# Order of the first projections: keys and queries ahead of values in the opening of a fused attention and gated-MLP kernel

## The chip, the cores and the metric

The kernel runs on one core of one Trainium2 chip. The metric is the device time of one execution in microseconds (us). The kernel before takes 264.70 us, the median of four runs (264.58 to 265.78 us). The profile comes from one further execution of the same kernel, which took 264.69 us; its span, from the first to the last instruction, is 262.9 us.

## The reference

Two branches, both fed with the normalised input, are added to the input; there are 2048 tokens of width 512:

```
xn  = layernorm(x)                              # 2048 x 512, no weights
q,k,v = xn @ wqkv                               # 32 heads of 16
s   = q k^T / 4, masked to 0 <= i - j < 256     # sliding window of 256 tokens
att = softmax(s) v @ wo
glu = ((xn @ w_gate) * (xn @ w_up)) @ w_down    # 512 -> 1792 -> 512
out = x + att + glu
```

All tensors are bf16; sums are kept in f32.

## The kernel before, in words

Tokens are worked in four chunks of 512 (`T` = 0 to 3), each of four blocks of 128 (`b`). For a chunk the kernel needs the normalised tokens transposed (`xnT`, model dimension on the partitions), keys, queries and values from `Wqkv`, 14 pairs of gate and up tiles, 15 or 20 batches of scores (exponentials on ScalarE, masks on GpSimd or VectorE), four groups of attention sums, and the sum of `Wd` and `Wo` products for the output.

TensorE (PE) writes to four PSUM banks `M0` to `M3` for everything but scores, and to `S` for scores. It works in four shapes of tile, which the trace names: 128*128 (dense products and transposes), 32*128 (scores, line 229), 64*17 (attention sums, line 259) and 128*64 (values, line 707).

The order of the instructions on every engine is not written out by hand. A planner in Python (class `Kernel`, `loop` at line 342, `choose` at line 373, `do` at line 433) runs while the program is built: it keeps a list `A` of dense pieces (class `Dense`, line 37: a name, a number of matmuls, what it depends on, a function that emits it and one that queues its copy out of PSUM), a list `B` of output sums, and counters for scores and attention sums. It estimates when each is ready, and emits the next one. It looks at the first `WINDOW` = 4 pieces of `A` (line 399), adds `SWITCH` = 0.11 when the tile shape would change (line 403), prefers a transpose ("turn") by 0.5 when it is ready soon (line 404), and starts an attention group between dense pieces under a rule with the age `now - 4` (line 389). Other engines' work (`Op`, line 26) is placed by `loop`, with a handicap `HOLD` before the first scores (line 351). So a changed cost or list can change the order of the whole program, though not the work.

The opening (`prologue`, line 150, and `first_chunk`, line 592) is special. Two queues load: ScalarE's x block 0 and two halves of a third of `Wqkv`; SyncE's x block 1, the other halves, then x block 2, 512 KB of `Wqkv`, x block 3, and everything later. `Wqkv` is 1536 columns wide: queries at 0, keys at 512, values at 1024. Loaded first are the values' columns, then the keys', then, behind x block 2, the queries'. Meanwhile 42 idle matmuls (`keep_busy`, line 207) run on PE. For each block VectorE takes the statistics (line 607, 609), ScalarE the square root (616), VectorE the reciprocal (619) and the normalised block `xn` (287); PE transposes it (640), and a copy brings it to `xnT` (647). Then PE makes, block by block, values (`add_v`, line 699), keys and queries (`project`, line 652: 16 matmuls of 128 columns each). Keys leave PSUM in two passes, one for each half of the heads' lanes (`i_keys`, line 290), queries and values in one.

Of the kernel before, what the change touches and what calls it, by code (L numbers as in the profile page):

```python
# [18 lines left out]
SWITCH = 0.11  # L19
# [17 lines left out]
class Dense:  # L37


    def __init__(self, name, mms, deps, emit, evac, mode="D"):  # L40
        self.name, self.mms, self.deps, self.emit, self.evac, self.mode = name, mms, deps, emit, evac, mode


# [47 lines left out]
class Kernel:  # L91
# [4 lines left out]
    PACE = 2.9  # L96
    SHARE = 1.0
    FEED = 0.1
    HOLD = 0.2

    def __init__(self, live=True):
        self.live = live
# [47 lines left out]
    def prologue(self):  # L150
        nc = self.nc
        xv = self.x_d.rearrange("(t p) d -> p t d", p=128)
        w = {k: v.rearrange("(k p) n -> p k n", p=128) for k, v in self.w_d.items()}

        def load(eng, dst, src):
            eng.dma_start(out=dst, in_=src)

        def qkv(eng, lo, k0, k1):
            load(eng, self.Wqkv[:, k0:k1, lo:lo + 512], w["qkv"][:, k0:k1, lo:lo + 512])

        load(nc.scalar, self.x[:, 0, :], xv[:, 0, :])
        load(nc.sync, self.x[:, 1, :], xv[:, 1, :])
        qkv(nc.sync, 1024, 0, 2)
        qkv(nc.scalar, 1024, 2, 4)
        qkv(nc.scalar, 512, 2, 4)
        qkv(nc.sync, 512, 0, 2)
        load(nc.sync, self.x[:, 2, :], xv[:, 2, :])
        qkv(nc.sync, 0, 0, 4)
        load(nc.sync, self.x[:, 3, :], xv[:, 3, :])
        h = self.F // 2  # L170
        for lo in (0, h):
            load(nc.sync, self.Wg[:, :, lo:lo + h], w["g"][:, :, lo:lo + h])
            load(nc.sync, self.Wu[:, :, lo:lo + h], w["u"][:, :, lo:lo + h])
            if lo == 0:
                load(nc.sync, self.x[:, 4:8, :], xv[:, 4:8, :])
        load(nc.sync, self.x[:, 8:NT, :], xv[:, 8:NT, :])
        for f, g in ((0, 5), (5, 10), (10, 14)):
            load(nc.sync, self.Wd[:, f:g], w["d"][:, f:g])
        load(nc.sync, self.Wo[:], w["o"])
        for _ in range(4):  # L180
            nc.sync.drain()

        c = self.const
        nc.gpsimd.memset(self.ident[:], 0.0)
        nc.gpsimd.affine_select(out=self.ident[:], in_=self.ident[:], compare_op=ALU.not_equal, fill=1.0,
                                base=0, pattern=[[-1, 128]], channel_multiplier=1)
        nc.gpsimd.memset(self.mhalf[:], -0.5)
        warm = c.tile([128, 1], F32, name="warm")
        nc.vector.memset(warm[:], 0.0)
        nc.vector.memset(self.eps[:], 1e-5)  # L190
        nc.scalar.activation(out=warm[:], in_=warm[:], func=ACT.Sqrt)
        self.warm = warm
        pi = c.tile([128, 1], I32, name="pi")
        nc.gpsimd.iota(pi[:], pattern=[[0, 1]], base=0, channel_multiplier=1)
        podd = c.tile([128, 1], I32, name="podd")
        nc.vector.tensor_scalar(out=podd[:], in0=pi[:], scalar1=4, scalar2=1,
                                op0=ALU.arith_shift_right, op1=ALU.bitwise_and)
        nc.vector.tensor_copy(out=self.own[:, 1:2], in_=podd[:])
        nc.vector.tensor_scalar(out=self.own[:, 0:1], in0=podd[:], scalar1=0, scalar2=None, op0=ALU.is_equal)
        nc.gpsimd.memset(self.V[0][:, :, :, 16:18], 1.0)  # L200
        for _ in range(4):
            nc.vector.drain()
        self.keep_busy(42, 0)

# [168 lines left out]
    def choose(self):  # L373

        now = self.now
        s = v = None
        more = self.g < len(self.batches)
        if more:
            s = early = self.when(self.score_deps(self.g))
            if s is not None and self.first_s is not None:  # L380
                s = max(s, self.first_s + self.PACE * self.g)
        free = sorted((t, i) for i, t in enumerate(self.banks) if t is not None)
        near, ready = False, None
        if self.v < len(self.pairs):
            near = self.of_pair[self.v][-1] < self.g
            v = ready = self.when(self.value_deps(self.v))
            if v is not None:
                v = max(v, free[1][0]) if len(free) > 1 else None
        if v is not None and v + 0.15 <= now and (self.mode == "S" or not more or s is None or s > now + 1.5 or v < now - 4):
            return now, "V", None  # L390
        if s is not None and s <= now:
            return now, "S", None
        cands = []
        if s is not None:
            cands.append((max(s, now), "S", None))
        if v is not None and (not more or s is None):
            cands.append((max(v, now), "V", None))
        a = b = None
        for n, d in enumerate(self.A[:self.WINDOW]):
            t = self.when(d.deps)  # L400
            if t is not None and free:
                t = max(t, free[0][0], now)
                t += SWITCH * (d.mode != self.mode) + SWITCH * (d.mode == "C" and self.mode == "D")
                t -= 0.5 * (d.name.startswith("turn") and t <= now + 0.4)
                if a is None or t < a[0]:
                    a = (t, n)
        if self.B and (self.B[0].T < NCH - 1 or not self.A):
            d = self.B[0]
            t = self.when(d.deps)
            if t is not None and ("bank" in d.link or free):  # L410
                b = max(t, now if "bank" in d.link else max(now, free[0][0]))
        held = near and len(free) < 3 and ready is not None and ready <= now + self.SOON
        if a is not None and held and (b is not None or cands):
            a = None
        if a is not None and b is not None:
            left = sum(x.hi - x.lo for x in self.B if x.T < NCH - 1)
            if max(a[0], b) <= now:
                kind = "B" if self.credit >= 1 and not left <= 5 else "A"
            else:
                kind = "A" if a[0] <= b else "B"  # L420
        else:
            kind = "A" if a is not None else "B" if b is not None else None
        if kind == "A":
            d = self.A[a[1]]
            a = (max(now, free[0][0], self.when(d.deps)), a[1])
            cands.append((a[0], "DA", a[1]))
        elif kind == "B":
            cands.append((b, "DB", None))
        if s is not None and early < s <= now + self.LEAD:
            cands.append((max(early, now) + 0.03, "S", None))  # L430
        return min(cands, key=lambda x: x[0]) if cands else None

    def do(self, at, kind, what):
        if at > self.now + 0.005:
            self.idle.append((self.now, at - self.now, kind))
        mode = self.A[what].mode if kind == "DA" else kind[0]
# [6 lines left out]
            self.do_values(at)  # L443
        elif kind == "DA":
            d = self.A.pop(what)
            i = self.take_bank()
            o = self.pe(at, d.mms * MM, d.name)
            if self.live:
                d.emit(i)
# [1 line left out]
            b = sum(x.hi - x.lo for x in self.B if x.T < NCH - 1)  # L451
            self.credit += d.mms * self.SHARE * b / max(sum(x.mms for x in self.A), 30)
        else:
            d = self.B[0]
# [136 lines left out]

    def first_chunk(self):

        land = (3.35, 3.4, 7.5, 9.6)
        wv, wk, wq = 5.6, 6.9, 9.2
        nc = self.nc
        roots = []
        for b in range(4):
# [9 lines left out]
                if n == halves - 1:  # L608
                    nc.vector.bn_aggr(out=self.mv[0][:, b, :], in_=keep["st"][:, 0:halves, :])  # L609

            deps = [land[b]]
            for n in range(halves):
                took = (0.72 if halves == 1 else 0.38) + (0.14 if n == halves - 1 else 0)
                s = self.op(f"st{b}", {"V": (took, took + 0.04)}, deps, lambda e, n=n, bn=bn: bn(e, n), rank=0.5)
# [20 lines left out]
        for b in range(4):  # L635
# [13 lines left out]
                self.at_["xnT", 0, b] = self.at_["xnT", 0, b, ks.start] = x  # L649
                x.then.append(lambda o: self.at_.update({("begun", 0, b, ks.start): o.start}))  # L650

            def project(i, lo, tok=tok):
                for k in range(4):
                    for c in range(4):
                        self.nc.tensor.matmul(  # L655
                            self.M[i][:, 128 * c:128 * c + 128], lhsT=self.Wqkv[:, k, lo + 128 * c:lo + 128 * c + 128],
                            rhs=self.xnT[0][:, k, tok], start=k + c == 0, stop=k == 3, skip_group_check=True)
# [14 lines left out]
                for c in range(4):  # L672
                    self.at_["Q", 0, c, b] = x

            at = len(self.A) - 2 if b else 0
            for n, ks in enumerate(([0, 1], [2, 3]) if b == 0 else ([0, 1, 2, 3],)):
                self.A.insert(at + n, Dense(f"turn{b}", 1.1 * len(ks) / 4, [("ap", b, n)], lambda i, f=turn, ks=ks: f(i, ks),
                                            lambda o, i, f=turned, ks=ks: f(o, i, ks)))
            self.add_v(0, b, wv)
            self.add(f"k0b{b}", 4.4, [("xnT", 0, b), wk], lambda i, f=project: f(i, 512), k_out)  # L680
            self.add(f"q0b{b}", 4.4, [("xnT", 0, b), wq], lambda i, f=project: f(i, 0), q_out)

    def norms(self, T):
        w = T % 2
# [14 lines left out]
    def add_v(self, T, b, land=0.0):  # L699
# [14 lines left out]
            self.frees(x, i)  # L714
            self.at_["V", T, b] = x

        x = [("xnT", T, b)] if T + b else [("xnT", 0, 0, 0), ("begun", 0, 0, 2)]
        self.add(f"v{T}.{b}", 4, x + [land] + self.ring(T, 2)[:1 if T == 3 else 0], emit, evac, "C")

    def add_qk(self, T, c):  # L720
# [130 lines left out]
```

The softmax here doesn't subtract the row's maximum and nothing guards it: scores larger than these inputs give would overflow.

## Time and profile before

| what | from | value |
|---|---|---|
| median of four runs | times | 264.70 us |
| the profiled execution | times | 264.69 us |
| its span | the page's first line | 262.9 us |
| PE busy | part 1 | 258.6 us, 98% of the span |
| VectorE, ScalarE, GpSimd busy | part 1 | 189.7, 165.4, 119.1 us |
| PE in the chain that ended last | part 4 | 96% |
| granted PE clock | cores | 1.000 |
| first real PE work (transpose of block 0) | timeline | 5.58 us |
| first scores | timeline | 17.03 us |
| last matmuls, end of the span | timeline | 259.9 us, 262.9 us |

Lines of the timeline give the start, the duration, the engine, the source line, the operation, what is written and read with its shape, the number of instructions merged in the line, and in brackets the idle time of that engine before them with what ended it. Matmuls are pipelined: the duration of a line runs to the modelled end of its last matmul, some 0.2 us after the next line may have started. So the pace of PE is read from one start to the next.

### The profile page before, as it was taken

The page shows a single profiled execution, that of the slowest core. Times are in us where ns is not written, and L with a number is a line of the kernel's source. Part 1 is how long each engine was busy: PE and PEld are TensorE (multiplying, and loading weights), DVE is VectorE, ACT ScalarE, POOL GpSimd, SP SyncE. Part 2 cuts the span into 40 slices and gives each one's busy share as a digit, 9 for nine tenths or more (in the row PEclk, how much of TensorE's full clock was granted, in tenths as well). Part 3 has the DMA queues.
Part 4 walks back from the last instruction along what each step waited for, and adds up shares of the span by engine and source line. Part 5 has one row for each costly group of instructions (what it writes and reads, how often), then busy time and mean ns, then how long its engine had stood idle before and what let it go on. Part 6 is the DMA issues. An engine that isn't in the chain of part 4 may idle for free.

```text
span 262.9 us, 8001 instructions
## 1 busy us (share of the span) xinstructions
PE 258.6 (98%) x3456; PEld 131.8 (50%) x3456; DVE 189.7 (72%) x367; ACT 165.4 (63%) x122; POOL 119.1 (45%) x274
## 2 busy tenths in 40 slices
PE   8999999999999999999999999999999999999995
PEld 7974444564444444546444444536535354544562
DVE  4889886969998277787999178777945459787504
ACT  3777676779567675677676756673886765674000
POOL 1046846483183918164282818163073636427000
PEclk9999999999999999999999999999999999999999
DMA  6999910000001300000004200000000100000002
GB/s 214 377 374 350 229 23 1 2 2 1 2 2 42 81 22 22 2 0 2 2 0 82 64 22 0 4 2 0 2 2 22 40 4 22 0 2 0 2 2 82
DMA packets 17252, 13.89 MB, mean 53 GB/s; under 512 B 7104, under 2 KB 17216, under 8 KB 17216
## 3 DMA queue, kind: packets, MB, share of 16 engines
q1 hardware_dynamic: 16384, 12.65, 17.6%
q10 hardware_dynamic: 832, 0.72, 0.8%
q8 instruction: 27, 0.44, 0.7%
q14 instruction: 9, 0.07, 0.1%
HBM read 9.70 MB, written 2.10 MB: 45 GB/s over the span
## 4 chain that ended last, share of the span: by engine, by line
PE 96%; DMA 2%; DVE 1%; issue 0%; ACT 0%
PE M L221 70%; PE S L229 9%; PE M L259 7%; PE M L707 6%; PE M L655 3%; DMA x<-in_A_x_dram 1%; DMA out_dram<-xn 1%; PE S L221 1%; DVE xn L801 1%; PE M L640 1%; DVE st L607 0%; DVE xn L287 0%; ACT ve L616 0%; PE M L211 0%; DVE mv L609 0%
## 5 line engine op out<-in xcount | busy, mean ns | idle before, releaser
L512 ACT ACTIVATE P<-S 128x2048 bf16<-128x2048 f32 x75 | 140.7, 1876 | 57.4 <-PE S L229 49.9
L238 POOL TENSOR_SCALAR_AFFINE_SELECT P<-P 64x256 bf16<-64x256 bf16 (+1 forms) x250 | 112.0, 450 | 111.0 <-ACT P L512 98.8
L221 PE MATMUL M<-xnT,Wu 128*128 128x512 bf16 x224 | 57.7, 380 | 0.0
L221 PE MATMUL M<-xnT,Wg 128*128 128x512 bf16 x224 | 57.7, 380 | 0.0
L221 PE MATMUL M<-Wd,hT 128*128 128x512 bf16 (+1 forms) x224 | 52.3, 373 | 0.0
L759 DVE TENSOR_TENSOR hT<-M,gsb 128x512 bf16<-128x512 f32 x56 | 38.1, 681 | 7.8 <-PE M L221 7.3
L217 DVE CAST gsb<-M 128x512 bf16<-128x512 f32 x44 | 30.2, 686 | 10.8 <-PE M L221 10.6
L221 PEld LDWEIGHTS <-Wu 128*128 128x128 bf16 x224 | 20.4, 98 | 25.2 <-issue 3.0
L221 PEld LDWEIGHTS <-Wg 128*128 128x128 bf16 x224 | 20.5, 98 | 24.8 <-issue 2.1
L221 PEld LDWEIGHTS <-hT 128*128 128x128 bf16 x238 | 21.3, 98 | 23.0 <-issue 2.7
L229 PE MATMUL S<-Q,K 32*128 32x320 bf16 (+4 forms) x720 | 29.9, 254 | 0.0
L550 DVE STREAM_TRANSPOSE at<-M 128x512 f32<-128x512 f32 x32 | 21.4, 699 | 11.6 <-PE M L259 11.4
L229 PEld LDWEIGHTS <-K 32*128 32x128 bf16 x720 | 12.0, 92 | 31.4 <-issue 30.2
L244 DVE TENSOR_TENSOR P<-P,masks 128x512 int16<-128x512 int16 x56 | 22.3, 404 | 5.8 <-ACT P L512 5.8
L221 PE MATMUL M<-xnT,Wqkv 128*128 128x512 bf16 x96 | 22.6, 380 | 0.0
L259 PE MATMUL M<-P,V 64*17 64x320 bf16 (+4 forms) x1440 | 19.5, 252 | 0.0
L801 DVE TENSOR_TENSOR y<-M,x 128x512 bf16<-128x512 f32 x12 | 8.2, 684 | 14.4 <-PE M L221 14.4
L259 PEld LDWEIGHTS <-V 64*17 64x17 bf16 x1440 | 17.0, 86 | 2.6 <-issue 0.8
L298 DVE TENSOR_SCALAR K<-M,own 128x512 bf16<-128x512 f32 x23 | 16.6, 742 | 2.3 <-PE M L221 1.6
L221 PE MATMUL M<-Wo,OT 128*128 128x512 bf16 (+1 forms) x64 | 15.9, 373 | 0.0
L707 PE MATMUL M<-Wqkv,xnT 128*64 128x256 bf16 x256 | 15.5, 274 | 0.0
L707 PEld LDWEIGHTS <-xnT 128*64 128x64 bf16 x256 | 13.4, 110 | 1.8 <-issue 1.5
(53 smaller groups left out, 146.7 us busy)
## 6 DMA issues: line engine op xcount, KB each, us to landing
Wg<-in_B_w_gate_dram SPq DMA_DIRECT2D x2, 896.0 KB, 9.8
Wu<-in_B_w_up_dram SPq DMA_DIRECT2D x2, 896.0 KB, 11.7
out_dram<-y SPq DMA_DIRECT2D x12, 128.0 KB, 1.7
Wd<-in_B_w_down_dram SPq DMA_DIRECT2D x2, 640.0 KB, 12.4
x<-in_A_x_dram SPq DMA_DIRECT2D x1, 1024.0 KB, 13.7
Wqkv<-in_A_wqkv_dram ACTq DMA_DIRECT2D x2, 256.0 KB, 5.1
Wqkv<-in_A_wqkv_dram SPq DMA_DIRECT2D x2, 256.0 KB, 4.7
Wqkv<-in_A_wqkv_dram SPq DMA_DIRECT2D x1, 512.0 KB, 6.3
```

The source lines that it names most:

```text
L217: self.nc.vector.tensor_copy(out=out, in_=in_)
L221: self.nc.tensor.matmul(ps, lhsT=a, rhs=b, start=first and n == 0, stop=last and n == len(pairs) - 1)
L229: self.nc.tensor.matmul(self.S[:, e, 64 * at:64 * (at + m)], lhsT=self.K[U % 3][rows, c, j].rearrange("p l t -> p (l t)"), rhs=self.Q[T % ...
L238: self.nc.gpsimd.affine_select(out=v, in_=v, pattern=[[0, 4], [0, n], [sign, 64]], base=0, fill=0.0, compare_op=ALU.is_gt if kind else ALU ...
L244: self.nc.vector.tensor_tensor(out=v, in0=v, in1=m, op=ALU.bitwise_and)
L259: self.nc.tensor.matmul(banks[lane][32 * e:32 * e + 17, 64 * q:64 * (q + m)], lhsT=self.V[U % 3][rows, j, 4 * c + e, 0:17], rhs=P[rows, e, ...
L298: self.nc.vector.tensor_scalar(out=out, in0=in_, scalar1=own, scalar2=None, op0=ALU.mult)
L512: ex = self.op(f"exp{g}", {"A": (took + 0.06, took + 0.18)}, [o], lambda e: self.nc.scalar.activation(out=P[:, :, 0:hi], in_=self.S[:, :, ...
L550: t = self.op(f"tr{v}", {"V": (0.63, 0.71)}, [o] + ts, lambda e, par=par: nc.vector.transpose(out=self.at[:, :, par, :], in_=self.M[banks[ ...
L707: self.nc.tensor.matmul(self.M[i][64 * lane:64 * lane + 64, 256 * jj:256 * jj + 256], lhsT=self.xnT[T % 2][:, k, tok], rhs=w[:, lane], sta ...
L759: x = self.op(f"u{T}.{f}", {"V": PSUM_COPY["V"]}, [o, ("gate", T, f)], lambda e: self.nc.vector.tensor_tensor(out=self.hT[T % 2][:, f, :], ...
L801: self.nc.vector.tensor_tensor(out=keep["y"][:, cols], in0=self.M[i][:, cols], in1=self.x[:, t, cols], op=ALU.add)
```

## The change

It reorders the loads and the pieces of the opening, and changes the planner's rules:

- Loads: the first third of `Wqkv` on the two queues is now the keys', the second the queries', both in halves; the values' 512 KB go behind x block 2 on SyncE's queue. Sizes and places in the queues stay as they were.
- Pieces: keys and queries of a block are emitted as two half pieces of 8 matmuls that share a bank (`link`). The list is now: keys and queries of blocks 0 and 1, values of 0 and 1, keys and queries of 2 and 3, values of 2 and 3, each transpose ahead of its block's keys.
- Planner: `HOLD` 0.2 to 0.3; the transposes' window 0.4 to 0.2; the age for an attention group 4 kept as `LATE`; the extra cost of entering the 128*64 shape kept as `ENTER` = 0.11; a window of seven pieces before the first scores; a new rule `stays`, which puts scores off by up to 1.2 while value pieces are ready.
- Estimates of landing times, and one `drain` fewer on VectorE, nine more on GpSimd, all before the first data arrive.

```diff
-        qkv(nc.sync, 1024, 0, 2)
-        qkv(nc.scalar, 1024, 2, 4)
+        qkv(nc.sync, 512, 0, 2)
         qkv(nc.scalar, 512, 2, 4)
-        qkv(nc.sync, 512, 0, 2)
+        qkv(nc.scalar, 0, 2, 4)
+        qkv(nc.sync, 0, 0, 2)
         load(nc.sync, self.x[:, 2, :], xv[:, 2, :])
-        qkv(nc.sync, 0, 0, 4)
+        qkv(nc.sync, 1024, 0, 4)
...
-        for _ in range(4):
+        for _ in range(9):
+            nc.gpsimd.drain()
+        for _ in range(3):
             nc.vector.drain()
...
-        if s is not None and s <= now:
+        if s is not None and s <= now and not (now < s + self.STAY and self.stays(now)):
             return now, "S", None
...
-        for n, d in enumerate(self.A[:self.WINDOW]):
+        for n, d in enumerate(self.A[:self.WINDOW + 3 * (self.first_s is None)]):
...
+    def stays(self, now):
+
+        if self.mode != "C" or not any(t is not None and t <= now for t in self.banks):
+            return False
+        ready = [self.when(d.deps) for d in self.A[:self.WINDOW] if d.mode == "C"]
+        return any(t is not None and t <= now for t in ready)
...
-            at = len(self.A) - 2 if b else 0
+            at, x = len(self.A), [("xnT", 0, b)]
...
-            self.add_v(0, b, wv)
-            self.add(f"k0b{b}", 4.4, [("xnT", 0, b), wk], lambda i, f=project: f(i, 512), k_out)
-            self.add(f"q0b{b}", 4.4, [("xnT", 0, b), wq], lambda i, f=project: f(i, 0), q_out)
+            for name, lo, deps, out in (
+                    ("k", 512, (x if b else [("xnT", 0, 0, 0), ("begun", 0, 0, 2)]) + [wk], k_out), ("q", 0, x + [wq], q_out)):
+                link, key = {}, (name, "half", b)
+                self.add(f"{name}0b{b}", 2.2, deps, lambda i, f=project, lo=lo: f(i, lo, (0, 1)),
+                         lambda o, i, key=key: self.at_.update({key: o.start}), "D", link)
+                self.add(f"{name}0b{b}", 2.2, deps + [key], lambda i, f=project, lo=lo: f(i, lo, (2, 3)), out, "D", link)
+
+            if b % 2:
+                self.add_v(0, b - 1, wv)
+                self.add_v(0, b, wv)
```

## Prediction

> **What bounds the kernel now.** I read the shares and the chain first, then PE's timeline, then VectorE's and the landings of the opening. The page:
>
> ```profile
> span 262.9 us, 8001 instructions
> PE 258.6 (98%) x3456; PEld 131.8 (50%) x3456; DVE 189.7 (72%) x367; ACT 165.4 (63%) x122; POOL 119.1 (45%) x274
> PE 96%; DMA 2%; DVE 1%; issue 0%; ACT 0%
> ```
>
> PE is 96% of the chain. Its own timeline tells whether it ever waits:
>
> ```profile
> 5.58 0.54 PE L640 MATMUL M<-ident,xn 128*128 128x128 bf16 x4 [0.43 <-DVE xn L287]
> 6.33 1.06 PE L707 MATMUL M<-Wqkv,xnT 128*64 128x256 bf16 x16
> 7.38 0.40 PE L640 MATMUL M<-ident,xn 128*128 128x128 bf16 x4
> 7.62 2.84 PE L655 MATMUL M<-xnT,Wqkv 128*128 128x128 bf16 x48
> 10.30 0.39 PE L640 MATMUL M<-ident,xn 128*128 128x128 bf16 x4
> ...
> 12.53 2.84 PE L655 MATMUL M<-xnT,Wqkv 128*128 128x128 bf16 x48
> 15.21 1.03 PE L221 MATMUL M<-xnT,Wg 128*128 128x512 bf16 x4
> 16.07 1.03 PE L221 MATMUL M<-xnT,Wu 128*128 128x512 bf16 x4
> 17.03 0.40 PE L229 MATMUL S<-Q,K 32*128 32x320 bf16 x8
> 17.36 2.81 PE L707 MATMUL M<-Wqkv,xnT 128*64 128x256 bf16 x48
> 20.11 0.40 PE L229 MATMUL S<-Q,K 32*128 32x320 bf16 x12
> ```
>
> The reader is to see starts (first column) that follow each other at the pace of the work, while the second column runs past the next start: 48 matmuls from 7.62 to 10.30, 0.0558 us each, and 48 again from 12.53 to 15.21. After 5.58 no line of PE carries an idle time. I went on to the end: a dense tile of four 512-column matmuls takes 0.864 us in each stage, every change of shape costs the same, and the last matmuls start at 259.6. So PE is full from 7.4 us on. Work on PE can be moved but not hidden, and there is no wait left to remove behind the opening.
>
> One place is held by something else, the second transpose at 7.38: its input is normalised until 7.32.
>
> ```profile
> 6.91 0.41 DVE L287 TENSOR_SCALAR xn<-x,mv,rs 128x512 bf16<-128x512 bf16 x1
> 7.44 0.69 DVE L217 CAST V<-M 128x512 bf16<-128x512 f32 x1
> 9.81 0.41 DVE L287 TENSOR_SCALAR xn<-x,mv,rs 128x512 bf16<-128x512 bf16 x1
> ```
>
> The landings, asked for issue by issue (median us from issue):
>
> ```profile
> Wqkv<-in_A_wqkv_dram ACTq DMA_DIRECT2D x1, 256.0 KB, 4.5
> Wqkv<-in_A_wqkv_dram SPq DMA_DIRECT2D x1, 256.0 KB, 4.1
> Wqkv<-in_A_wqkv_dram ACTq DMA_DIRECT2D x1, 256.0 KB, 5.8
> Wqkv<-in_A_wqkv_dram SPq DMA_DIRECT2D x1, 512.0 KB, 6.3
> ```
>
> Issued at 1.24, 1.26, 1.73 and 2.74, they are in by 5.7, 5.3, 7.5 and 9.0 us.
>
> **What the Trainium skill says.** (1) "TensorEngine Tiling (Array Packing)", Key Properties: changing the tiling mode drains the array. The trace agrees and gives the price: gate to up (15.21 to 16.07) is 0.864 us, up to scores (16.07 to 17.03) 0.959: 0.095 us. Leaving the value shape costs 0.098, leaving the scores 0.093. I take 0.095. (2) "TensorE: Matmul & The Clock Gate", Part 1: the clock falls back after an idle window of about 3.4 us. Here the clock is granted from 4.61 us to the end, across 0.43 us of idling at 5.14. (3) "Trainium Kernel Development and Optimization", Key Constraints: DMAs of all queues share 16 engines. No run here shows whose bytes a slot carries to matter; sizes and order of slots decide.
>
> **The change part by part.** Numbers are against the profiled execution: 264.69 us, a span of 262.9 and 1.8 around it; it lies 0.01 us from the median 264.70.
>
> Loads. Every slot keeps its size, queue and place; only columns change. So I keep the landings: keys 5.3 and 5.7, queries 7.1 and 7.5, values 9.0, x block 3 at 9.4. Nothing is moved past another issue. Cost zero, and the cover is the slack below.
>
> Up to the second transpose. Values of block 0 (1.05 us from 6.33 to 7.38, both shape changes and a wait of some 0.05 in it) give way to keys of block 0: 16 x 0.0558 = 0.893 us, 6.33 to 7.23. The transpose still waits for `xn` at 7.32, as everything ahead of that on VectorE and ScalarE is in the same order. It starts at 7.38 again, after 0.15 us idle. Gain zero; if the cover of that wait were gone, 0.155 us gained.
>
> From the second transpose on. PE's work of the opening that is left was 3 blocks of values and 8 of keys or queries; now it is 4 and 7. A value block in a row is (2.744 - 0.098)/3 = 0.882 us, a key block 0.893: -0.01 us. What remains is shape changes. I counted them in the trace's order and in the order the changed program is built in. Before: opening dense, scores, 3 values, scores: 3 changes to the second batch of scores. After: dense to the value pair (between transposes 3 and 4), back, to scores, to the two other values, to a dense tile, to scores: 6. Through the rest the planner's new rules cost +1: in the second chunk an attention group now follows scores directly (-1), in the third one stands between dense tiles (+1), and ahead of the last chunk a dense tile comes between values and scores (+1). Whole program: 173 changes before, 175 after; two of the 173 lay ahead of the second transpose, where they were free, none of the 175. So +4 changes, 4 x 0.095 = +0.38 us.
>
> Do the moved pieces find their inputs? By row: third transpose at 7.38 + 0.23 + 2.68 = 10.30; values from 10.30 + 0.22 + 0.095 = 10.61, which need the columns of 9.0 (slack 1.6); fourth transpose at 10.61 + 2 x 0.882 + 0.098 = 12.48; 64 key and query matmuls of blocks 2 and 3 from 12.70; gate tile at 16.27, scores at 18.09. Block 2's `xn` must be ready by 10.24. VectorE: a key pass (0.74) instead of the values' copy (0.69) from 7.44, statistics to 8.97, then, new ahead of the reciprocal, the queries' copy (0.66) to 9.6, reciprocal at 9.5, `xn` 9.7 to 10.1. ScalarE: `xnT` to 8.42, second key pass (0.69) to 9.04, root to 9.3. That leaves 0.1 us; bounds 0 and +0.3 (one pass of 0.69 not hidden by 0.4), I take 0. Block 3's `xn` ends by the same rows at 12.25 against 12.42. Queries of the second block wait for a 256 KB half at its fifth matmul, 7.84, against 7.54. Block 3's `xnT` copy moves from ScalarE to VectorE: no row has it there; nearest are 0.24 (half as wide) and 0.69; it has 1.6 us until its keys start, so zero. The exponentials' table load (1.28) sits between two query copies of which the second ends near 17.2, 0.8 ahead of the scores.
>
> Later order. The scores come 1.06 us later and stay spaced by 3.0 us, or 2.6 in the output stages, as before; one exponential is 1.88. The attention group before the last chunk moves 3.2 us later; its banks' next use is 2.1 us off for two transposes of 1.31 in sum. Behind the opening, banks are reused after 1.2 us or more of PE time in both orders (a copy takes 0.69). I see no new wait: zero, with bounds 0 and +0.9 (a copy of 0.69 that queues once, with its latency). The tail, from the last scores on, has the same order. Drains and estimates: VectorE is idle until 3.70 and GpSimd until 12.56, where they stand; zero.
>
> Sum: 0 - 0.01 + 0.38 + 0 = +0.37; 264.69 + 0.37 = 265.06 us.
>
> **Rivals.** (A) Forecast: four shape changes more, no new wait: 265.06. (B) The keys' earlier end frees the second transpose: it would need `xn` by 7.17, and the change leaves VectorE's order there alone. Gain 0.155: 264.9 us. (C) Copies pile up at transposes 3 or 4, or once later: for it, slacks of 0.1 and 0.2 us; against it, all rows used are measured. 0.2 to 0.9: 265.3 to 266.0, say 265.6. (D) Slower: the values' 512 KB come later than the slot's 9.0 us. Everything on PE stands behind the value matmuls at 10.61, in order, so each us past that is one us. It passes 0.5% when they land at 11.6 or later; at 12.6 it gives 267.1. For it: 350 GB/s flow in that stretch and the slot is behind three others; against it: same bytes in the same slots, slack 1.6. (E) Faster by over 0.5% would need 1.3 us of PE idle removed; only 0.43 at 5.14 and the tail exist, and neither is touched.
>
> **How the numbers follow.** A 0.70, B 0.09, C 0.09, D 0.10, E 0.02. A measurement of this kernel can tell about 0.5% (1.3 us) from no change: A, B and C lie within. Faster 0.02, same 0.88, slower 0.10. A's own range is 264.8 to 265.4; the range 264.5 to 266.0 takes in B and C with the bounds above and the spread of single runs, and leaves D and E out.
>
> **What would show it.** Second transpose still at 7.4 after an idle PE; third near 10.3, values near 10.6, first scores near 18.1 with no idle time on PE; 0.86 and 0.96 us paces unchanged; last matmul 0.37 later. Wrong if PE lines after 7.4 carry idle time, if the values' landing passes 10.6, or if the second transpose moves ahead of 7.3.

## The result and the profile after

The changed kernel takes 265.01 us, the median of 42 runs (264.74 to 265.81). In the same sessions the kernel before takes 264.76 us (64 runs, 264.41 to 265.78). The ratio is 1.001, with a 95% interval of 1.0005 to 1.0014: slower by 0.25 us, well within the 0.5% that the forecast set as the bound of a change, where the forecast had 0.37 us. The profiled execution took 264.92 us.

The page of the changed kernel, in the lines that answer to those shown of the kernel before:

```profile
span 263.2 us, 8016 instructions
PE 259.2 (98%) x3456; PEld 131.8 (50%) x3456; DVE 188.9 (72%) x366; ACT 166.2 (63%) x123; POOL 119.8 (46%) x274
PE 96%; DMA 2%; DVE 1%; issue 0%; ACT 0%
```

PE runs the same 3456 matmuls, is busy 0.6 us longer and is still 96% of the chain. The bound is the same. Next is PE's timeline in the opening of the changed kernel (start, duration, line, what is written and read, count, and in brackets an idle time ahead):

```profile
6.21 1.06 PE L670 MATMUL M<-xnT,Wqkv 128*128 128x128 bf16 x16
7.26 0.40 PE L655 MATMUL M<-ident,xn 128*128 128x128 bf16 x4
7.49 2.84 PE L670 MATMUL M<-xnT,Wqkv 128*128 128x128 bf16 x48
10.17 0.39 PE L655 MATMUL M<-ident,xn 128*128 128x128 bf16 x4
10.49 1.94 PE L729 MATMUL M<-Wqkv,xnT 128*64 128x256 bf16 x32
12.36 0.40 PE L655 MATMUL M<-ident,xn 128*128 128x128 bf16 x4
12.59 3.74 PE L670 MATMUL M<-xnT,Wqkv 128*128 128x128 bf16 x64
16.17 1.03 PE L228 MATMUL M<-xnT,Wg 128*128 128x512 bf16 x4
...
17.99 0.40 PE L236 MATMUL S<-Q,K 32*128 32x320 bf16 x8
```

The reader is to see the order of the change, with no bracket from 7.26 us on. The forecast had the third transpose at 10.30, the values at 10.61, the fourth transpose at 12.48, the gate tile at 16.27 and the first scores at 18.09. Each stands here 0.10 to 0.13 us earlier, because in this execution the whole opening does: VectorE's first statistics start at 3.58 us here and at 3.70 in the profile before. Asked for all waits of PE, the trace of the changed kernel answers with two lines, both ahead of the second transpose (time, number, longest):

```profile
PE M L218 <- PEq L857: 0.8, 1, 0.8
PE M L655 <- DVE xn L294: 0.2, 1, 0.2
```

VectorE's timeline of the changed kernel shows why the second transpose hasn't moved, and the copy that the forecast had no row for:

```profile
6.79 0.41 DVE L294 TENSOR_SCALAR xn<-x,mv,rs 128x512 bf16<-128x512 bf16 x1
7.30 0.75 DVE L305 TENSOR_SCALAR K<-M,own 128x512 bf16<-128x512 f32 x1
...
12.79 0.42 DVE L224 COPY xnT<-M 128x512 bf16<-128x512 bf16 x1 [0.40 <-PE M L655]
```

The normalised block is ready at 7.20, the transpose starts at 7.26, and the 16 key matmuls that began at 6.21 end their pace near 7.10 (16 x 0.0558): PE waits some 0.15 us, as forecast. The full-width copy of `xnT` on VectorE takes 0.42 us, between the 0.24 and the 0.69 of the forecast. The 512 KB that now carry the values land as they did with other columns, 6.3 us after their issue, at 9.07, 1.42 us ahead of the value matmuls:

```profile
Wqkv<-in_A_wqkv_dram SPq DMA_DIRECT2D x1, 512.0 KB, 6.3
```

To compare the two traces without the shift of the opening, I read from the start of the second transpose to the start of the last matmul, and call this the stretch. Before: 7.385 to 259.608, which is 252.223 us. After: 7.259 to 259.923, which is 252.664. So the path that PE sets is 0.44 us longer, where the forecast had 0.37. Up to the start of the second batch of scores it is +1.176 us, of which one gate tile more (0.864) has only been moved ahead: +0.312 for three changes of shape. The rest of the program adds +0.129, for one. What is left, from the last matmul's start to the end of the span, is the tail: 3.27 us before and 3.28 after.

### The profile page after: what moved, and what is told of

It reads as the page before. It is cut to its first block, busy times and chain, and to the rows that moved or that the text cites. A ratio compares the mean times of both kernels' runs of the same rounds, so it can differ in the third digit from the quotient of the medians.

```text
span 263.2 us, 8016 instructions
## 1 busy us (share of the span) xinstructions
PE 259.2 (98%) x3456; PEld 131.8 (50%) x3456; DVE 188.9 (72%) x366; ACT 166.2 (63%) x123; POOL 119.8 (46%) x274
## 4 chain that ended last, share of the span: by engine, by line
PE 96%; DMA 2%; DVE 1%; issue 0%; ACT 0%
PE M L228 70%; PE S L236 9%; PE M L266 7%; PE M L729 6%; PE M L670 3%; DMA x<-in_A_x_dram 1%; DMA out_dram<-xn 1%; PE S L228 1%; PE M L655 1%; DVE xn L823 1%; DVE st L622 0%; DVE xn L294 0%; ACT ve L631 0%; PE M L218 0%; DVE mv L624 0%
## 5 line engine op out<-in xcount | busy, mean ns | idle before, releaser
L224 DVE CAST gsb<-M 128x512 bf16<-128x512 f32 x39 | 26.7, 685 | 6.1 <-PE M L228 5.7
L305 DVE TENSOR_SCALAR K<-M,own 128x512 bf16<-128x512 f32 x24 | 17.2, 741 | 3.5 <-PE M L228 2.5
L222 ACT ACTIVATE gsb<-M 128x512 bf16<-128x512 f32 x17 | 10.2, 598 | 8.7 <-PE M L228 7.7
```

Source lines behind the costliest of these rows:

```text
L224: self.nc.vector.tensor_copy(out=out, in_=in_)
L305: self.nc.vector.tensor_scalar(out=out, in0=in_, scalar1=own, scalar2=None, op0=ALU.mult)
```

## The experiments

### The planner's rules and the new order, apart

The forecast took three of the four added shape changes from the new opening and one from the planner's new rules. The first experiment keeps the changed opening and puts the old rules back:

```diff
-    HOLD = 0.3
-    TURN = 0.2
-    STAY = 1.2
+    HOLD = 0.2
+    TURN = 0.4
+    STAY = 0.0
...
-        for n, d in enumerate(self.A[:self.WINDOW + 3 * (self.first_s is None)]):
+        for n, d in enumerate(self.A[:self.WINDOW]):
```

> The new opening with the planner's old rules (HOLD 0.2, TURN 0.4, no stay, window 4). As built it has 175 shape changes, as the changed kernel has. If shape changes alone set the time: from the second transpose to the last matmul 252.67 us as in the changed kernel (252.23 before), 0.2 to 0.4 us over before in the median, no idle time on PE after that transpose. If the later extra change came from the new rules, as the prediction put it: 0.1 us less than the changed kernel.

Measured: 265.21 us (22 runs), ratio 1.0014 (1.0007 to 1.0022). Its program has 175 changes, as the changed kernel has, and behind the opening PE's order is the changed kernel's. So the fourth change doesn't come from the rules. The stretch is 252.87 us, 0.21 more than in the changed kernel: two starts are late, the third transpose by about 0.07 us and one batch of scores at 213.72 by 0.155 us (its exponential stood behind a mask of GpSimd; why, I haven't settled).

The second experiment is the other half, the new rules on the old opening (`HOLD`, `TURN`, `STAY`, the wider window and `stays`):

> The old opening with the planner's new rules alone. As built it has 173 shape changes, as before. If shape changes alone set the time: 252.23 us from the second transpose to the last matmul and a median equal to before within 0.1 us. If the rules cost by themselves: 0.1 us or more over before.

Measured: 266.12 us (6 runs), ratio 1.0045 (1.0030 to 1.0060), far more than the rules were thought to cost. 173 changes of shape are left, as before. The stretch is 252.61 us, +0.39 against the kernel before; the tail is 4.25 us, +0.98. Two separate things, then. The first is a wait that the rules bring to the old opening; the second returns below with the drains, and to take it out I ran the same kernel with one drain less on VectorE:

```diff
-        for _ in range(4):
+        for _ in range(3):
             nc.vector.drain()
```

> The new rules in the old opening, as in the kernel that took 266.1 us, with three drains on VectorE (445 instructions there instead of 446). If the fetch made its tail long: back to 3.3 us from the last matmul's start to the end, and 0.3 to 0.4 us remain over before, the waits of PE at 9.7 and 11.0 us that the trace of that kernel shows: some 265.2. If not: 266.1 again.

Measured: 265.19 us (12 runs), ratio 1.0003 (0.9992 to 1.0015). The stretch is 252.62 us, +0.39 again, the tail 3.28. PE's timeline of this kernel shows the wait, which ends with a key pass of ScalarE (L300); ScalarE's timeline follows:

```profile
10.20 0.39 PE L651 MATMUL M<-ident,xn 128*128 128x128 bf16 x4
10.82 1.95 PE L666 MATMUL M<-xnT,Wqkv 128*128 128x128 bf16 x32 [0.24 <-ACT K L300]
```

```profile
9.51 1.26 ACT L300 ACTIVATE K<-M,own 128x512 bf16<-128x512 f32 x2 [0.33 <-PE M L666]
```

From transpose to projection it is 0.62 us here and 0.22 in the kernel before. The bank that PE waits for is freed by the second key pass of block 0. In the kernel before, ScalarE makes both passes of block 0 one after the other, and the bank is free at 10.16. In this program the first went to VectorE, and the second stands on ScalarE behind a pass of block 1; it is the second of the two in the line, and ends at 10.77. So the rules make a late copy in the old order and, by these profiles, spare 0.2 us of late starts in the new one. They belong to the order that they came with; neither half has a value of its own that could be added up.

### The price of a change of shape

Is 0.095 us per change, read off neighbouring starts, what a change costs the whole program? Two kernels add one small matmul of 64 columns ahead of each of the 14 up tiles of the second chunk. Its result is overwritten. In one kernel it has the value shape, which makes 23 changes more; in the other it has the shape of its neighbours:

```diff
+            if T == 1 and W is self.Wu:
+                ones = self.nc.const_aps.tensor(1.0, [128, 128], BF16)
+                self.nc.tensor.matmul(self.M[i][0:64, 0:64], lhsT=ones[:, 0:64], rhs=ones[:, 0:64], start=True, stop=True,
+                                      tile_position=(0, 0), skip_group_check=True)
```

> The kernel before with one extra matmul of 64 columns in the 128*64 shape ahead of each of the 14 up tiles of the second chunk; its result is overwritten. As built it has 196 shape changes, 23 more. At 0.095 us each and some 0.03 us for each matmul: 23 x 0.095 + 14 x 0.03 = 2.6 us over before. If a shape change costs only where weights or data wait: 0.4 us.

> The same 14 extra matmuls in the 128*128 shape of their neighbours, no shape change more. 14 x 0.03 to 0.06 = 0.4 to 0.8 us over before. The difference to the kernel with 23 changes more is 23 x 0.095 = 2.2 us if shape changes cost 0.095 us; 0 if it is the extra matmul that costs.

Measured: 267.90 us (4 runs), ratio 1.0118 (1.0072 to 1.0164), with the other shape; 265.15 us (12 runs), ratio 1.0011 (0.9997 to 1.0024), with the same shape. PE's timeline, first with the value shape, then with the neighbours' shape:

```profile
64.38 1.03 PE L221 MATMUL M<-xnT,Wg 128*128 128x512 bf16 x4
65.33 0.22 PE L750 MATMUL M<-const-bfloat16-1.0 128*64 128x64 bf16 x1
65.48 1.04 PE L221 MATMUL M<-xnT,Wu 128*128 128x512 bf16 x4
```

```profile
64.11 1.03 PE L221 MATMUL M<-xnT,Wg 128*128 128x512 bf16 x4
64.97 0.19 PE L750 MATMUL M<-const-bfloat16-1.0 128*128 128x64 bf16 x1
65.00 1.03 PE L221 MATMUL M<-xnT,Wu 128*128 128x512 bf16 x4
```

Gate to up is 1.10 us in the first and 0.89 in the second. Over the program the stretch is 2.99 and 0.40 us longer than in the kernel before: 14 short matmuls cost 0.029 us each, and the remaining 2.59 us, if the short matmul itself takes the same time in both shapes, are 0.113 for each of 23 changes. Nothing hides them: a change on a PE that never waits is paid in full. This is a little above 0.095: in the lines shown, entering the short matmul costs 0.09 more with the other shape (0.95 instead of 0.86) and leaving it 0.12 more (0.15 instead of 0.03).

### Values that come late

Rival D said that each microsecond by which the values pass their start on PE is a microsecond of the whole. The changed kernel's 512 KB of value weights were put behind the first half of the gate weights:

```diff
-        qkv(nc.sync, 1024, 0, 4)
...
+            if lo == 0:
+                qkv(nc.sync, 1024, 0, 4)
```

> The changed kernel with the values' 512 KB moved from behind x block 2 to behind the first half of the gate weights, so that they land near 11.9 instead of 9.1 us. The value matmuls start at 10.49 in the changed kernel. If PE stands in order behind them: idle until 11.9, the whole time grows by 1.4 us to 266.4. If the 1.4 us between landing and use in the changed kernel were not slack but hid something: another number.

Measured: 266.44 us (9 runs), ratio 1.0057 (1.0040 to 1.0073). In its profile (an execution of 266.91 us) the values land at 12.46, where 11.9 was expected, and PE's timeline says what that does:

```profile
12.50 1.94 PE L730 MATMUL M<-Wqkv,xnT 128*64 128x256 bf16 x32 [1.66 <-DMA Wqkv<-in_A_wqkv_dram]
```

Counted from the second transpose, the value matmuls start 1.85 us later than in the changed kernel, and the stretch is 1.83 us longer: one for one, and nothing behind made it up.

The other kernel keeps the old order of the work, values first, and takes only the new order of the loads (the first hunk of the diff, in the kernel before):

> The kernel before, its order kept, with the loads of the change: values of block 0 stay first on PE but their columns come in the last slot, at 9.0 us. If PE takes its work strictly in order and has no slack behind: they start at 9.1 instead of 6.33, and the whole time grows by the same 2.75 us, to 267.5. If later idle time takes some of it up: less.

Measured: 269.46 us (2 runs, 268.92 and 269.99), ratio 1.0170 (1.0139 to 1.0200), where the waiting alone (2.86 us) would give 267.7. PE's timeline of this kernel, and then its stretches by window (length, busy time of PE, its weight loads, VectorE, ScalarE, GpSimd, then the granted clock, DMA share, GB/s):

```profile
9.20 1.92 PE L707 MATMUL M<-Wqkv,xnT 128*64 128x256 bf16 x16 [3.06 <-DMA Wqkv<-in_A_wqkv_dram]
11.05 0.61 PE L640 MATMUL M<-ident,xn 128*128 128x128 bf16 x4
11.45 4.29 PE L655 MATMUL M<-xnT,Wqkv 128*128 128x128 bf16 x48
```

```profile
4.00:7.60 3.60, 1.75 (x22) 1.36 (x21) 2.72 (x11) 0.97 (x3) 0.00 (x0) 1.00 1.06 354
7.60:9.20 1.60, 0.01 (x2) 0.00 (x1) 0.00 (x0) 0.00 (x0) 0.00 (x0) 0.52 1.08 377
9.20:14.50 5.30, 5.30 (x49) 4.92 (x49) 1.64 (x4) 1.70 (x4) 0.00 (x0) 0.50 1.07 376
```

The values wait 3.06 us, and PE's clock falls to one half at 7.65 us, in the middle of that, and stays there until 14.48. From the start of one line to the next, the 16 value matmuls take 1.85 us instead of 1.05, the transpose 0.40 instead of 0.23, and the 48 matmuls 4.13 instead of 2.68. That is a second price, 0.80 + 0.17 + 1.45 = 2.42 us, on top of the 2.86 us by which the values start later (9.20 instead of 6.33); together 5.28, and the span is 268.2 us instead of 262.9. The forecast priced a late load at one for one without a limit; that holds for the 1.66 us of the kernel above, where the clock stayed at 1.00, and not for the 3.06 us here. "TensorE: Matmul & The Clock Gate", Part 1 of the Trainium skill gives an idle window of about 3.4 us; here the clock fell 1.5 us into an idle stretch of 3.06 us that followed 22 sparse matmuls, so an idle time under that figure isn't safe.

Nor does the length of the wait alone tell the two kernels apart. In this profile the full clock held for 3.413 us (4.24 to 7.65) and the half clock for twice that; in the other 13 profiles the full clock held for 75, 76 or 77 times 3.413 us. So in these traces the clock changes in steps of that length. In the step that ends with the fall, PE was busy for 1.51 us of 3.41. In the kernel above, the whole wait of 1.66 us lies in one step (10.74 to 14.15, counted on from the first grant at 3.91), with PE busy for 1.75 us of 3.41, and the clock stayed. The wait took less of its step here (6.14 to 7.65, 1.51 us) than there, so the sparse matmuls ahead of it seem to have counted too. No run tests that apart, or says where the limit lies.

### The drains

The forecast put one `drain` fewer on VectorE and nine more on GpSimd at nothing, since both engines are idle where they stand. First both edits alone, in the kernel before:

> The kernel before with the changed drains alone (nine on GpSimd, three instead of four on VectorE). They stand where those engines are idle: equal to before within 0.1 us, 252.23 us from the second transpose to the last matmul. A rival, that instruction fetches shift: any difference above 0.1 us, with idle time on an engine that has none before.

Measured: 264.98 us (14 runs), ratio 1.0005 (0.9996 to 1.0014): nothing that can be told. But the tail of the rules' kernel was 0.98 us longer with PE's work long done, and its last two outputs landed late. That kernel differs from the one before at its end only in the length of the engines' instruction streams, so I varied only that: one VectorE drain more, and eight more, in the kernel before.

```diff
-        for _ in range(4):
+        for _ in range(5):
             nc.vector.drain()
```

> The kernel before with one drain more on VectorE (five instead of four) and nothing else. PE's work and order are those of before: 252.2 us from the second transpose to the last matmul. If the tail of the kernel with the new rules was long because VectorE's 446th instruction moves an 8 KB instruction fetch into the landing of the last output: the tail from the last matmul's start to the end grows from 3.27 to some 4.2 us, and the median is 0.9 us over before. If it was something else in that kernel: equal to before within 0.1 us.

> The kernel before with twelve drains on VectorE, seven more than the last one. If the place of the fetch decides, it now lies ahead of the last output, in VectorE's idle time before the tail: 3.3 us or less of tail, a median within 0.1 us of before. If more instructions on VectorE lengthen the tail as such: 4 us or more of tail.

Measured: five drains 265.71 us (20 runs), ratio 1.0027 (1.0019 to 1.0035); twelve drains 264.79 us (20 runs), ratio 0.9995 (0.9984 to 1.0005). One instruction that costs nothing where it stands makes the kernel 0.7 to 0.8 us slower (0.84 between the medians, 0.71 by the ratio, 0.73 in the tail), and eight of them don't. PE is untouched: the stretch with five drains is 252.222 us, the same as before to 1 ns. Then the two halves of the edit in the changed kernel: the fourth VectorE drain put back, and the nine GpSimd drains taken out.

> The changed kernel with VectorE's fourth drain put back (446 instructions there instead of 445). If the drain taken away in the change pays for a semaphore wait that the new order adds on VectorE: tail of 4.2 us instead of 3.28, a median near 266.0. If the drains cost and bring nothing, as the prediction said: equal to the changed kernel within 0.1 us.

> The changed kernel without the nine drains on GpSimd (306 instructions there instead of 315). If they bring nothing: equal to the changed kernel within 0.1 us, 265.0. If a fetch of GpSimd falls in the tail too: a tail longer than 3.28 us.

Measured: with the fourth drain 265.83 us (20 runs), ratio 1.0034 (1.0024 to 1.0043); without GpSimd's nine 265.33 us (12 runs), ratio 1.0012 (1.0002 to 1.0022). The first is clear against the changed kernel's 1.0010 (1.0005 to 1.0014), the second isn't.

What takes the time is seen in the landings of the last outputs, the two of 64 KB (KB each, median us from issue to landing). First the kernel before, then the same with five drains; there the line of the queue q14 above them gives packets, MB and share.

```profile
out_dram<-xn SPq DMA_DIRECT2D x1, 64.0 KB, 1.6
out_dram<-xn ACTq DMA_DIRECT2D x1, 64.0 KB, 1.6
```

```profile
q14 instruction: 2, 0.02, 1.2%
...
out_dram<-xn SPq DMA_DIRECT2D x1, 64.0 KB, 2.4
out_dram<-xn ACTq DMA_DIRECT2D x1, 64.0 KB, 2.3
```

In the changed kernel, too, both take 1.6; in the changed kernel with four drains 2.3. The queue q14 carries instructions: in these last microseconds two packets of 8 KB, each 0.3 to 0.7 us long. The table sets their place against the end of the issue of the last output, whose packets run from about 0.5 to 0.9 us after it. The counts are of VectorE's stream in the built program.

| kernel | VectorE instructions | fetches, us after the last issue | last outputs, us | tail, us |
|---|---|---|---|---|
| before, three drains (and GpSimd's nine) | 444 | 1.07 | 1.6, 1.6 | 3.58 |
| before | 445 | 0.94, 1.08 | 1.6, 1.6 | 3.27 |
| changed | 445 | 0.85, 0.95 | 1.6, 1.6 | 3.28 |
| changed, no GpSimd drains | 445 | 0.85, 0.92 | 1.6, 1.6 | 3.25 |
| rules, three drains | 445 | 0.82, 1.03 | 1.6, 1.6 | 3.28 |
| rules, four drains | 446 | 0.59, 0.85 | 2.6, 2.6 | 4.25 |
| before, five drains | 446 | 0.24, 0.84 | 2.4, 2.3 | 4.00 |
| changed, four drains | 446 | 0.23, 0.89 | 2.3, 2.3 | 4.02 |
| before, twelve drains | 453 | -2.39, 0.91 | 1.6, 1.6 | 3.27 |

All three kernels with 446 VectorE instructions have a fetch ahead of or amid the last outputs' packets, and in all three 8 of the 128 packets of each output, a sixteenth, come after all its others, the last of them 0.3 to 0.7 us after these. With 445 the fetches start when nearly all of the packets have been sent; with 453 one of them is over before the outputs; with 444 the outputs are in time, but the last instructions of GpSimd and VectorE start 0.3 to 0.4 us later than elsewhere, and what they wait for isn't settled. The five other profiles fit: four kernels with 445 have outputs of 1.6 us and tails of 3.26 to 3.29, and the new opening with the old rules, at 443, has 1.6 and 3.34. That the place of the fetch goes with the count and that the late outputs go with the place is shown. That the fetch holds up one of the 16 DMA engines, and with it that engine's share, is argued from the sixteenth: the trace doesn't name the engine of a packet.

## Why the prediction was right, and where it wasn't

The time (265.06 us) and the side were right, and by the mechanism named: four changes of shape more on a PE that is never idle. That the forecast and the median (265.01) lie only 0.05 us apart is in part luck, since the stretch grew by more than forecast and the medians differ by less. By its steps:

- **Loads at no cost.** Right: same slots, landings within 0.31 us of those before (the keys' half on SyncE moved most, 5.32 to 5.63), and 1.42 us between the values' landing and their use. The two late-value kernels show that this slack was what mattered.
- **Second transpose pinned by `xn`.** Right. In every kernel whose clock is full by then and whose values aren't late it starts 3.67 to 3.69 us after VectorE's first statistics. What scatters it from run to run is the landing of x block 0, which puts the first statistics at 3.40 to 3.83 us over the profiles. Rival B falls.
- **Four changes of shape, +0.38.** The count is right, and the stretch grew by 0.44. The opening's three came to 0.312 where the sum had 0.275, the later one to 0.129 instead of 0.095. Part of it is a term that was left out: the first pair of matmuls of a value block behind a change takes 0.130 us instead of 0.106, and there is one such entry more behind the second transpose (0.024). Some 0.05 us stays open. The medians are only 0.25 us apart (0.13 to 0.37 by the interval). In the profiles the difference is an opening that began 0.12 us earlier; whether that belongs to the change or to the scatter of x block 0, these runs can't tell.
- **One of the four "from the planner's new rules".** Wrong in the cause: with the old rules the later order and its 175 changes are the same. The cause is the new opening: with it alone the planner takes the other order. That it does so because the first scores come 1.08 us later is likely, but not shown. What the rules do is spare 0.2 us of late starts, 0.07 of it at the third transpose.
- **No new wait (C).** Right: no bracket behind the second transpose. The slack of 0.1 us at the third transpose held with the new rules; with the old ones it missed by 0.07.
- **Drains at nothing.** Right as a sum, wrong as a reason. "Idle where they stand" isn't enough: dropping the VectorE drain is worth 0.6 to 0.8 us in the changed kernel (265.83 with the drain; 0.74 in the tail). With the drain VectorE's stream would have 446 instructions in the changed order; without it, it stays at 445. Had the change kept the drain, the forecast would have missed by nearly 0.8 us and nothing in its sum would have said why. That this term came out at zero is luck. GpSimd's nine showed no effect.
- **Rival D, one for one.** Right at 1.66 us of waiting, too low in the kernel with 3.06, where the halved clock adds 2.4.

## What to carry to other kernels

When one engine is full from end to end, price a new order by what it makes that engine do: count the changes of tile shape in the built order, multiply by the step between neighbouring starts, and look for one pinned start ahead of which work is free. A late load in front of such an engine cost its lateness one for one here, and more where the clock fell as well. Before believing a difference under one microsecond, compare the stretch of the bounding engine and the tail apart: a shift in the number of instructions, through drains that do nothing, can lengthen the tail by more than the change under study.

## What the runs showed of the hardware that was not expected

- In the three kernels with an instruction fetch of 8 KB ahead of or amid the packets of the last 64 KB outputs, the end came 0.7 to 1.0 us later, and one instruction more or less on VectorE decided it. "Runtime: NRT & Kernel Launch", Instruction fetch mechanics of the Trainium skill calls the cost of fetching the next block of instructions mostly hidden; in the tail of these three kernels it doesn't look hidden.
- The full clock was granted at times from 3.67 to 6.82 us in these profiles, with the same 42 idle matmuls ahead in each. Where it came after 6.4 us (two profiles), the second transpose started 3.87 and 3.94 us after the first statistics instead of 3.68.
- The clock changed in steps of 3.413 us. It fell to one half after a step in which PE was busy for 1.51 us, and stayed full through one with 1.75 us.
